# Batch 1's x on SyncE's queue, 1 KB pieces of x for every batch, and three more staging buffers in the first layer

## The chip, the cores and the metric

The kernel runs on one core of a Trainium2 chip. The metric is the device time of one execution in microseconds. Engines by their names in the profile: PE is TensorE, DVE is VectorE, ACT is ScalarE, POOL is GpSimd, SP is SyncE (which here only issues DMAs).

## What is computed

Four batches of attention between 512 tokens and 32 state rows (8 heads of 64), read in both directions, then two feed-forward layers over all 2304 rows:

```python
a  = softmax(scale * x @ state.T);  xread = a  @ state      # per batch and head
a2 = softmax(scale * state @ x.T);  sread = a2 @ x
x1 = concat(xread, sread)                                   # 4 batches x (512 + 32) rows, 512 wide
h  = x1 @ w_in;  x2 = (h - tanh(h)) @ w_out                 # 512 -> 2048 -> 512
h  = x2 @ w2_in; out = (h * tanh(softplus(h))) @ w2_out
```

The four weight matrices come as 64-bit floats, 8 MB each, so every tile of 128x512 weights is a load of 512 KB that has to be converted on the chip.

## The kernel before, in words

**Weights.** `load_next` (lines 161 to 170) issues one load of 512 KB on SyncE's queue into a staging buffer; there are three (pool `stage`). `conv_steps` (line 172) converts a loaded tile in three steps: ScalarE reads the high words (tile `w`), ScalarE reads the low words (tile `r`) and then the next load is issued, and VectorE joins the two. Where a weight is used in three matmuls of the fp32r type (all but the first `PLAIN` = 3 tiles of w_out), `split` makes a high part on ScalarE and a low part on VectorE (`wh`, `wl`; `gh`, `gl` for activations). Loads of the first layer alternate: four tiles of w_in, then w_in and w_out in turn, 32 in all.

**First layer, batch by batch.** The state is multiplied into w_in first (`sw`, `sw_first`; tiles `swh`, `swl`), so that the attention weights a (transposed and split: `ath`, `atl`, by `at_a_hi` and `at_a_lo`) meet it directly. For each batch, step t of 16 does `up_x` (6 matmuls into `h`, then tanh into `t` on ScalarE, a subtraction on VectorE, a split) and, three steps later (`LA`), `down_x` (12 matmuls into the four `acc` banks; 4 plain ones for the first three tiles). In batch 0's 16 steps the weights are converted too, two tiles a step; after every fourth step `sw` needs four new tiles of w_in. After batch 0 all weights stay in place. The second layer follows, block by block.

**Start.** `FIRST_LOADS` is the order of the first loads on SyncE's queue: `s` and `t` are the two states, a digit is one quarter of a batch's x (0 to 3 batch 0), `w` a weight tile. `FIRST_STEPS` is an order written out by hand: while `Pinned.on` is set, TensorE, ScalarE and VectorE each execute their instructions strictly in the order of this list, up to the bar; behind it the scheduler orders them by priority and readiness. The letters stand for the functions in `steps` (line 892): `x`/`X` transpose and copy a quarter of batch 0's x, `p`/`P` of batch 1's; `c`/`C` and `q`/`Q` are the scores and their copies for batches 0 and 1; `t m b e u v y` the softmax of batch 0; `h`/`l` the attention weights transposed and split; `f` the product of state and w_in; `w` one step of a weight's conversion; `k` matmuls on zeros; `L` issues batch 1's x on GpSimd's queue behind VectorE's last instruction.

**Layout of x.** A quarter of a batch's x holds two heads. Batch 0's comes in 1 KB pieces (four tokens of a head), so that one transposed 128x128 block holds two tokens of one head, on partitions 0 to 63 and 64 to 127. `sc_first` therefore needs each head's state on both halves of the partitions, in `SB` and, swapped, in `SX`. Batches 1 to 3 come in pieces of 256 bytes on GpSimd's queue, with the two heads side by side, and `sc_m` takes matmuls of 512 columns.

**Slots.** 97 slots of 128x512 are handed out by `get` and taken back by `put`, oldest first.

## Time and profile before

| | us |
|---|---|
| median of 3 runs | 756.31 (755.75 to 756.71) |
| the profiled execution, its own time | 755.38 |
| its span, first to last instruction | 753.6 |
| TensorE busy in the span | 732.3 |
| VectorE / ScalarE / GpSimd busy | 537.0 / 417.6 / 16.2 |

The profile is one execution on the core. A row of a timeline has its start and duration in us; behind a row, in brackets, stands how long the engine had been idle and what released it. `L56` is the line of the helper that records every operation, so the tiles' names tell which operation it is: `out<-in`. In groups, `busy, mean ns | idle before <-releaser` follow the count.

### The profile page before, as it was taken

Reading aid. Unit: us, or ns where it says so; the run is one execution under the profiler, and the core shown is the slowest. Engines: PE = TensorE matmul, PEld = TensorE weight load, DVE = VectorE, ACT = ScalarE, POOL = GpSimd, SP = SyncE. Lnnn points to the kernel's source line nnn. Section 1 sums busy time; section 2 is a strip of 40 time slices with the busy share of each in tenths; the row PEclk is TensorE's granted clock in tenths of the full one; section 3 lists DMA queues with packets and bytes.
Section 4 is the critical chain, followed back from the end, with each engine's and each line's share of the span. In section 5 each row is a group of like instructions: output and inputs, shape, how many; then the busy total and the mean of one; then the engine's idle time right before and its main releaser. Section 6 shows DMA issues by size and latency. Waiting matters only on the chain.

```text
span 753.6 us, 10473 instructions
## 1 busy us (share of the span) xinstructions
PE 732.3 (97%) x4108; PEld 593.1 (79%) x4108; DVE 537.0 (71%) x989; ACT 417.6 (55%) x779; POOL 16.2 (2%) x18
## 2 busy tenths in 40 slices
PE   7889899999999999999999999999999999999997
PEld 5546687678777788777888888888888888899996
DVE  3657865664447444677698987878887888788896
ACT  4789844544545543688774644445444454545563
POOL 3000020000200000000000000000000000000000
PEclk9899999999999999999999999999999999999999
DMA  8477720000200200253410000100010000100100
GB/s 246 146 239 242 230 56 1 2 1 30 84 29 29 85 29 29 78 159 128 140 57 1 0 1 2 56 1 0 1 57 0 1 1 0 57 1 1 43 1 28
DMA packets 16400, 43.13 MB, mean 57 GB/s; under 512 B 2656, under 2 KB 5728, under 8 KB 16352
## 3 DMA queue, kind: packets, MB, share of 16 engines
q1 hardware_dynamic: 15392, 39.33, 16.2%
q0 software_dynamic: 960, 3.15, 1.7%
q8 instruction: 32, 0.52, 0.3%
q14 instruction: 16, 0.13, 0.1%
HBM read 38.01 MB, written 4.46 MB: 56 GB/s over the span
## 4 chain that ended last, share of the span: by engine, by line
PE 87%; DMA 5%; ACT 4%; DVE 3%; issue 0%; POOL 0%; SPq 0%; ACTq 0%
PE acc L56 45%; PE h L56 36%; DMA st<-in_moe_w_in_dram 3%; DMA x<-in_x_dram 2%; PE swp L56 2%; ACT w L56 1%; ACT r L56 1%; DMA st<-in_moe_w_out_dram 1%; PE srd L56 1%; PE xtp L56 1%; DVE swl L56 1%; PE atp L56 1%; PE e2p L56 1%; ACT gh L56 0%; PE sct L56 0%; ACT t L56 0%
## 5 line engine op out<-in xcount | busy, mean ns | idle before, releaser
L56 PE MATMUL h<-yl,wh 128*128 128x512 f32 (+2 forms) x320 | 114.4, 358 | 0.0
L56 PE MATMUL h<-yh,wl 128*128 128x512 f32 (+2 forms) x320 | 114.4, 358 | 0.0
L56 PE MATMUL h<-yh,wh 128*128 128x512 f32 (+2 forms) x320 | 114.3, 357 | 0.0
L56 PE MATMUL acc<-wl,gh 128*128 128x512 f32 x288 | 112.5, 391 | 0.0
L56 PE MATMUL acc<-wh,gh 128*128 128x512 f32 x288 | 112.5, 390 | 0.0
L56 PE MATMUL acc<-wh,gl 128*128 128x512 f32 x288 | 112.4, 390 | 0.0
L56 ACT ACTIVATE er<-er 128x512 f32<-128x512 f32 (+2 forms) x136 | 75.8, 557 | 42.7 <-DVE er L56 40.6
L56 PE MATMUL acc<-gh,wh 128*128 128x512 f32 x244 | 99.0, 406 | 0.0
L56 ACT ACTIVATE er<-h 128x512 f32<-128x512 f32 (+2 forms) x68 | 35.5, 522 | 109.5 <-PE h L56 108.4
L56 PE MATMUL acc<-gh,wl 128*128 128x512 f32 x244 | 95.5, 391 | 0.0
L56 PE MATMUL acc<-gl,wh 128*128 128x512 f32 x244 | 95.1, 390 | 0.0
L56 DVE TENSOR_TENSOR t<-h,t 128x512 f32<-128x512 f32 x68 | 46.8, 688 | 65.5 <-ACT t L56 65.3
L56 DVE SCALAR_TENSOR_TENSOR er<-er 128x512 f32<-128x512 f32 (+2 forms) x136 | 81.3, 598 | 4.7
L56 ACT ACTIVATE t<-h 128x512 f32<-128x512 f32 x68 | 40.6, 597 | 70.8 <-PE h L56 70.5
L56 PEld LDWEIGHTS h<-yh,wh 128*128 128x128 f32 x320 | 60.3, 188 | 8.9
L56 PEld LDWEIGHTS h<-yl,wh 128*128 128x128 f32 x320 | 60.3, 188 | 8.9 <-DVE yl L56 0.4
L56 PEld LDWEIGHTS h<-yh,wl 128*128 128x128 f32 x320 | 60.3, 188 | 7.5
L56 PEld LDWEIGHTS acc<-wh,gl 128*128 128x128 f32 x288 | 54.0, 188 | 11.5
L56 PEld LDWEIGHTS acc<-wh,gh 128*128 128x128 f32 x288 | 54.1, 188 | 11.4 <-ACT t L56 0.8
L56 PEld LDWEIGHTS acc<-wl,gh 128*128 128x128 f32 x288 | 54.1, 188 | 10.2
L56 PEld LDWEIGHTS acc<-gh,wh 128*128 128x128 f32 x244 | 45.8, 188 | 18.9 <-issue 6.5
L56 DVE SCALAR_TENSOR_TENSOR w<-w,r 128x512 uint32<-128x512 uint32 x64 | 44.0, 689 | 21.6 <-ACT r L56 17.1
(100 smaller groups left out, 1204.3 us busy)
## 6 DMA issues: line engine op xcount, KB each, us to landing
st<-in_moe_w_in_dram SPq DMA_DIRECT2D x32, 512.0 KB, 4.4
st<-in_moe_w_out_dram SPq DMA_DIRECT2D x32, 512.0 KB, 4.1
out_dram<-o SPq DMA_DIRECT2D x16, 256.0 KB, 2.2
x<-in_x_dram POOLq DMA_DIRECT2D x12, 256.0 KB, 4.3
x<-in_x_dram SPq DMA_DIRECT2D x4, 256.0 KB, 4.0
stt<-in_state_dram SPq DMA_DIRECT2D x2, 128.0 KB, 5.1
out_dram<-o SPq DMA_DIRECT2D x4, 64.0 KB, 1.7
```

The costliest lines, as they stand in the source:

```text
L56: i = fn(*args, **kw)
```

## The change

Batch 1's x is loaded on SyncE's queue behind the first two weights and the second state, and the x of all batches comes in 1 KB pieces; batches 2 and 3 stay on GpSimd's queue. All scores are computed as batch 0's were, with the swapped state `SX` now for both states in a slot, copied by VectorE. The hand-written start is reordered: weight 0 and 1 are converted earlier, and `f` is divided into `f` (matmul and high part) and `g` (low part). The slots fall to 91; the memory of six of them makes three staging buffers `wide`, which take loads 3, 4, 5, then 9, 10, 11 and so on of the first layer's weights, so that six loads go out at the start instead of three. When batch 1's layer starts, `widen` hands their six halves out as slots; `get` takes a half first for 32-bit float tiles.

```diff
--- before.py
+++ after.py
@@ -15,6 +15,7 @@
 AX = mybir.AxisListType
 LA = 3
+WIDE = 3
 RESERVE = 10
 E20 = 485165195.40979
 REBIAS = 2.0 ** -112
@@ -28,10 +29,12 @@
-FIRST_LOADS = "s0123wwwt"
+FIRST_LOADS = "s0123wwt4567wwww"
 FIRST_STEPS = """
-    k4 s0 x0 X0 x1 X1 x2 X2 x3 X3 L c0 C0 C1 k2 t0 m0 t1 b0 w0 w0 m1 e0 w1 b1 w0 k8 e1 w1 u0 p0
-    P0 p1 P1 f0 v0 y0 p2 P2 u1 v1 h0 p3 P3 y1 k4 h1 l0 w1 l1 w2 q1 Q0 Q1 | f1 w2 w2 f2 w3 w3 w3 f3
+    k4 s0 x0 X0 x1 X1 x2 X2 x3 X3 w0 w0 c0 C0 C1 k2 w0 t0 m0 t1 w1 w1 f0 b0 p0 P0 m1 e0 p1 P1 b1
+    p2 e1 P2 u0 p3 P3 v0 y0 k6 w2 u1 v1 w2 h0 q1 y1 k2 h1 g0 l0 w1 l1 Q0 Q1 | f1 g1 w2 f2 g2
+    w3 w3 w3 f3 g3
 """
 BLOCKS = [4, 4, 4, 3, 2]
@@ -101,16 +104,24 @@
     slots = ctx.enter_context(tc.tile_pool(name="slots", bufs=1))
     psum = ctx.enter_context(tc.tile_pool(name="psum", bufs=1, space=bass.MemoryType.PSUM))
-    NSLOT = 97
-    free = deque(range(NSLOT))
+    NSLOT = 97 - 2 * WIDE
+    free, halves = deque(range(NSLOT)), deque()
+    wide = [slots.tile([128, 1024], F32, tag=f"v{i}", name="wide") for i in range(WIDE)]
     def get(name, dtype=F32, newest=False):
+        if halves and dtype == F32:
+            return halves.popleft()
         i = free.pop() if newest else free.popleft()
         return Unit(slots.tile([128, 512], dtype, tag=f"k{i}", name=name), i)
     def put(*units):
         for u in units:
-            free.append(u.slot)
+            if u.slot is None:
+                halves.append(u)
+            else:
+                free.append(u.slot)
     ps_n = [0]
     banks = ["s0", "s1", "a0", "a1", "a2", "a3", "h0", "h1"]
@@ -124,11 +135,12 @@
     XS = get("xst")
     xst = XS.t.rearrange("p (k n) -> p k n", k=KD)
-    SX = misc.tile([128, KD * NS], F32, name="sx")
-    def head(b, k, i):
+    SX = get("sx")
+    def head(b, k, i, half=None):
         c = (b * KD + k) * NS
-        return SB.t[i * 64:(i + 1) * 64, c:c + NS]
+        p = i if half is None else half
+        return (SB if p == i else SX).t[p * 64:(p + 1) * 64, c:c + NS]
     def by_head(name, b, rhs):
@@ -155,6 +167,7 @@
     last = [None]
+    loads = [-1]
     pending = deque()
     raws = {}
@@ -162,7 +175,11 @@
         if not pending:
             return
         key, src = pending.popleft()
-        t = stage.tile([128, 1024], U32, tag="st", name="st")
+        loads[0] += 1
+        if key[0] in ("w1i", "w1o") and loads[0] % (3 + WIDE) >= 3:
+            t = wide[loads[0] % (3 + WIDE) - 3].bitcast(U32)
+        else:
+            t = stage.tile([128, 1024], U32, tag="st", name="st")
         if key[:2] == ("w1i", 0):
             nc.sync.dma_start(out=t.rearrange("p (k c) -> p k c", k=KD), in_=src)
         else:
@@ -240,25 +257,17 @@
     X, A, AT = {}, {}, {}
     XT, SC, ET = {}, {}, {}
-    def load_x(b, ks=range(KD), after=None):
+    def load_x(b, ks=range(KD)):
         for k in ks:
             u = get("x", newest=b > 1)
-            if b:
-                dma = nc.gpsimd.dma_start(
-                    out=u.t.rearrange("p (r h d) -> p r h d", r=4, h=2),
-                    in_=x[b, 2 * k:2 * k + 2].rearrange("h (p r) d -> p r h d", r=4),
-                )
-                if after is not None:
-                    order(dma.ins, after, mybir.DependencyClass.Sync)
-            else:
-                nc.sync.dma_start(
-                    out=u.t.rearrange("p (h c) -> p h c", h=2),
-                    in_=x[b, 2 * k:2 * k + 2].rearrange("h (p r) d -> p h (r d)", r=4),
-                )
+            (nc.gpsimd if b > 1 else nc.sync).dma_start(
+                out=u.t.rearrange("p (h c) -> p h c", h=2),
+                in_=x[b, 2 * k:2 * k + 2].rearrange("h (p r) d -> p h (r d)", r=4),
+            )
             X[b, k] = u
     def x_tile(b, k, i, r):
-        c = r * 128 + i * 64 if b else i * 256 + r * 64
+        c = i * 256 + r * 64
         return X[b, k].t[:, c:c + 64]
     P = {}
@@ -283,44 +292,35 @@
         xt_t(b, k)
         xt_c(b, k)
-    def sc_first():
-        P["c"] = [side_bank("sct") for _ in range(2)]
+    def sc_m(b):
+        P["c", b] = [side_bank("sct") for _ in range(2)]
         before = None
         for i in range(2):
             for k in range(KD):
                 for e in range(2):
                     with tc.high_priority() if before else nullcontext():
                         mm = TE.matmul(
-                            out=P["c"][e][k * NS:(k + 1) * NS, i * 256:(i + 1) * 256],
-                            lhsT=head(0, k, i) if e == i
-                            else SX[e * 64:(e + 1) * 64, k * NS:(k + 1) * NS],
-                            rhs=XT[0, k].t[e * 64:(e + 1) * 64, i * 256:(i + 1) * 256],
+                            out=P["c", b][e][k * NS:(k + 1) * NS, i * 256:(i + 1) * 256],
+                            lhsT=head(b, k, i, e),
+                            rhs=XT[b, k].t[e * 64:(e + 1) * 64, i * 256:(i + 1) * 256],
                             start=True,
                             stop=True,
                         ).ins
                     if before:
                         order(mm, before)
                     before = mm
-        put(*(XT.pop((0, k)) for k in range(KD)))
-    def sc_first_c(i):
-        SC[0, i] = get("scs")
+        put(*(XT.pop((b, k)) for k in range(KD)))
+    def sc_c(b, i):
+        SC[b, i] = get("scs")
         for e in range(2):
             evac(
-                SC[0, i].t.rearrange("p (q e n) -> p q e n", q=2, e=2)[:, :, e, :],
-                P["c"][e][:, i * 256:(i + 1) * 256].rearrange("p (q n) -> p q n", q=2),
+                SC[b, i].t.rearrange("p (q e n) -> p q e n", q=2, e=2)[:, :, e, :],
+                P["c", b][e][:, i * 256:(i + 1) * 256].rearrange("p (q n) -> p q n", q=2),
                 e,
             )
-    def sc_m(b):
-        P["c", b, 0], P["c", b, 1] = by_head("sct", b, [[XT[b, k].t for k in range(KD)]])
-        put(*(XT.pop((b, k)) for k in range(KD)))
-    def sc_c(b, j):
-        SC[b, j] = get("scs")
-        AC.activation(out=SC[b, j].t, in_=P.pop(("c", b, j)), func=ACTF.Copy)
     def at_scores(b):
         sc_m(b)
@@ -487,13 +487,17 @@
                 put(SB)
     def sw_first(f):
-        ps = by_head("swp", 0, [[w1i_tile(0, k, f) for k in range(KD)]])
+        P["f", f] = ps = by_head("swp", 0, [[w1i_tile(0, k, f) for k in range(KD)]])
         for j in range(2):
             if f == 0:
                 SW[0, 0, j] = (get("swh", F32R), get("swl", F32R))
+            h = SW[0, 0, j][0].t[:, f * 128:(f + 1) * 128]
+            AC.activation(out=h, in_=ps[j], func=ACTF.Copy)
+    def sw_first_lo(f):
+        for j, ps in enumerate(P.pop(("f", f))):
             h, l = (u.t[:, f * 128:(f + 1) * 128] for u in SW[0, 0, j])
-            AC.activation(out=h, in_=ps[j], func=ACTF.Copy)
-            V.tensor_tensor(out=l, in0=ps[j], in1=h.bitcast(F32), op=ALU.subtract)
+            V.tensor_tensor(out=l, in0=ps, in1=h.bitcast(F32), op=ALU.subtract)
     def mm3p(o, lh, ll, rh, rl, start, stop):
@@ -853,12 +857,10 @@
                 in_=ps[p].rearrange("p (e i n) -> p e i n", i=2, n=NS)[:, :, i, :],
                 func=ACTF.Copy,
             )
-            if g == 0:
-                AC.activation(
-                    out=SX[p].rearrange("p (k n) -> p k n", n=NS),
-                    in_=ps[p].rearrange("p (e i n) -> p e i n", i=2, n=NS)[:, :KD, 1 - i, :],
-                    func=ACTF.Copy,
-                )
+            V.tensor_copy(
+                out=SX.t[p, g * 256:(g + 1) * 256].rearrange("p (e n) -> p e n", n=NS),
+                in_=ps[p].rearrange("p (e i n) -> p e i n", i=2, n=NS)[:, :, 1 - i, :],
+            )
         put(u)
     nc.scalar.preload_act_table_set("exp_and_others")
@@ -891,10 +893,11 @@
     steps = {
         "x": lambda k: xt_t(0, k), "X": lambda k: xt_c(0, k), "s": lambda j: state_t(j, st[j]),
-        "c": lambda j: sc_first(), "C": sc_first_c, "t": lambda j: sc_t(0, j),
+        "c": lambda j: sc_m(0), "C": lambda j: sc_c(0, j), "t": lambda j: sc_t(0, j),
         "m": lambda j: sc_max(0, j), "b": lambda j: sc_sub(0, j), "e": lambda j: sc_exp(0, j),
         "u": lambda j: nm_sum(0, j), "v": lambda j: nm_rec(0, j), "y": lambda j: nm_mul(0, j),
         "h": lambda j: at_a_hi(0, j), "l": lambda j: at_a_lo(0, j), "f": sw_first,
+        "g": sw_first_lo,
         "w": conv_first, "k": keep_warm, "p": lambda k: xt_t(1, k), "P": lambda k: xt_c(1, k),
         "q": sc_m, "Q": lambda j: sc_c(1, j),
     }
@@ -904,13 +907,17 @@
         if key == "|":
             for e in (TE, AC, V):
                 e.floor, e.on = e.last, False
-        elif key == "L":
-            load_x(1, after=V.recent)
         else:
             steps[key[0]](int(key[1:]))
     put(warm)
     at(4, lambda: state_t(1, st[1]))
     banks[2:] = []
+    def widen():
+        for t in wide:
+            put(*(Unit(t[:, h * 512:(h + 1) * 512], None) for h in range(2)))
+    at(start[1], widen)
     def up(q):
         if q[0] == "x":
```

## Rows read from the trace of the kernel before

**Rows 1.** The page: totals of the engines, and the span in 40 equal slices.

```profile
PE 732.3 (97%) x4108; PEld 593.1 (79%) x4108; DVE 537.0 (71%) x989; ACT 417.6 (55%) x779; POOL 16.2 (2%) x18
...
PE   7889899999999999999999999999999999999997
...
DMA  8477720000200200253410000100010000100100
```

**Rows 2.** Busy time by window: engine busy us (instructions), PEclk, DMA share, GB/s.

```profile
0.00:10.00 10.00, 7.92 (x72) 5.84 (x72) 1.87 (x3) 3.56 (x7) 1.42 (x7) 1.00 0.79 243
...
7.50:10.00 2.50, 2.22 (x36) 1.00 (x36) 0.69 (x1) 0.30 (x1) 0.73 (x1) 1.00 1.04 347
...
10.00:25.00 15.00, 11.52 (x110) 9.20 (x108) 9.53 (x20) 8.48 (x17) 4.55 (x4) 0.77 0.66 171
...
12.50:15.00 2.50, 1.55 (x13) 1.15 (x11) 2.47 (x5) 2.17 (x4) 2.05 (x2) 1.00 0.91 178
...
20.00:25.00 5.00, 4.88 (x53) 3.92 (x52) 3.56 (x8) 2.80 (x5) 0.00 (x0) 0.71 0.02 8
...
25.00:86.10 61.10, 51.55 (x283) 32.69 (x268) 42.38 (x71) 53.87 (x104) 0.00 (x0) 1.00 0.72 232
...
86.10:753.60 667.50, 661.28 (x3664) 545.39 (x3662) 483.25 (x897) 351.69 (x654) 10.22 (x8) 1.00 0.11 36
```

**Rows 3.** The chain of waits, 0 to 100 us: its shares, then pieces (start us, us, what).

```profile
by line: DMA st<-in_moe_w_in_dram 20.6%; DMA x<-in_x_dram 12.6%; ACT w L56 8.8%; ACT r L56 8.5%; DMA st<-in_moe_w_out_dram 8.2%; PE acc L56 8.0%; PE h L56 4.1%; ACT gh L56 3.2%; PE xtp L56 2.6%; ACT t L56 2.1%; POOL x L247 1.9%; issue 1.7%;
...
11.16 7.82 DMA x<-in_x_dram
...
88.29 2.76 PE acc L56 x12
...
91.05 1.36 PE h L56 x6
```

**Rows 4.** Timeline of TensorE: start us, us, operation [idle before <-releaser].

```profile
7.58 0.66 PE L56 MATMUL xtp<-ident,x 128*128 128x128 f32 x4 [0.41 <-DMA x<-in_x_dram]
...
13.88 0.63 PE L56 MATMUL xtp<-ident,x 128*128 128x128 f32 x4 [0.46 <-DMA x<-in_x_dram]
...
19.11 1.09 PE L56 MATMUL xtp<-ident,x 128*128 128x128 f32 x4 [0.94 <-DMA x<-in_x_dram]
...
25.12 0.50 PE L56 MATMUL h<-ath,swh 128*128 128x512 f32 x1
...
80.08 1.09 PE L56 MATMUL swp<-w,sbt 64*32 64x512 f32 x16 [1.32 <-DVE w L56]
...
85.81 0.66 PE L56 MATMUL sc<-ident,scs 128*128 128x128 f32 x4 [1.69 <-DVE swl L56]
...
86.22 0.48 PE L56 MATMUL h<-ath,swh 128*128 128x512 f32 x1
```

**Rows 5.** Timelines of GpSimd, VectorE and SyncE, 9 to 28 us.

```profile
9.27 5.28 POOL L247 DMA_DIRECT2D x<-in_x_dram  x4 [7.97 <-DVE xt L56]
...
10.15 0.76 DVE L56 COPY scs<-sct 128x256 f32<-128x256 f32 x2 [1.18 <-PE sct L56]
...
27.08 0.34 SPq L169 DMA_DIRECT2D st<-in_moe_w_out_dram  x1
```

**Rows 6.** Groups of ScalarE's instructions, 10 to 25 us and 25 to 86.1 us.

```profile
L56 ACT ACTIVATE xt<-xtp 128x512 f32<-128x512 f32 x4 | 2.4, 592 | 3.7 <-PE xtp L56 3.7
...
L56 ACT ACTIVATE w<-st 128x512 f32<-128x512 f32 x29 | 19.8, 682 | 7.0 <-DMA st<-in_moe_w_in_dram 6.4 <-DMA st<-in_moe_w_out_dram 0.4
```

**Rows 7.** Waits of SyncE's queue, 0 to 95 us: us in total, times, longest.

```profile
SPq L169 <- ACT r L56: 57.4, 30, 11.4
```

**Rows 8.** Timelines of ScalarE and VectorE about 120 us.

```profile
120.42 0.60 ACT L56 ACTIVATE t<-h 128x512 f32<-128x512 f32 x1 [1.45 <-PE h L56]
...
122.44 0.69 DVE L56 TENSOR_TENSOR gl<-t,gh 128x512 fp32r<-128x512 f32 x1 [0.70 <-ACT gh L56]
```

## The prediction, made before the changed kernel ran

> **What bounds the kernel now.** I read the page's totals and slices first [rows 1]. TensorE is busy for 732.3 of 753.6 us, and its line of tenths is at 9 nearly everywhere except in the first five slices, some 90 us. In those same slices the DMA line stands at 7 and 8. So what can be gained cheaply lies ahead of 90 us. The windows confirm it [rows 2]: from 86.1 us to the end TensorE is busy for 661.28 of 667.50 us, 6.2 us idle in all, while from 25 to 86.1 us it is busy for 51.55 of 61.10 us, 9.55 us idle. The chain of waits over the first 100 us [rows 3] then says which resource it is: the loads of the first layer's weights hold 20.6% and 8.2% of it, x another 12.6%, and TensorE's matmuls for acc and h only 8.0% and 4.1%. This stretch is led by transfers, in two parts.
>
> *Part one, up to 25 us.* The first up-projection matmul starts at 25.12 us [rows 4]. What it waits for is a line of small steps written out by hand, and batch 1's four transposes stand in the middle of that line. They are held by batch 1's x: the piece of the chain that begins at 11.16 us is one x transfer of 7.82 us [rows 3], and the transposes start at 13.88 and 19.11 us, each released by a landing [rows 4]. GpSimd issues these four loads only at 9.27 us [rows 5]. ScalarE meanwhile sits idle for 3.7 us ahead of the copies of those transposes [rows 6]. While the 256-byte pieces move, the DMA engines are nearly full (0.91) yet carry 178 GB/s, against 347 GB/s in the window before them [rows 2]. Then, from 20 to 25 us, the engines carry 8 GB/s at a share of 0.02 [rows 2]: all three staging buffers are full, and SyncE's next load goes out at 27.08 us [rows 5], since ScalarE reaches weights 2 and 3 late.
>
> *Part two, 25 to 86.1 us.* The DMA share is 0.72 [rows 2]. SyncE waits 30 times, 57.4 us together, for ScalarE's second read of a staging buffer (r) [rows 7], then the load needs time to land, and ScalarE in turn idles 7.0 us ahead of its first read (w), 6.8 us of it named as those loads [rows 6]. That is a ring of three buffers in which each side waits for the other.
>
> **The change, part by part.**
>
> *Front.* Batch 1's x moves from GpSimd's queue, with a wait on VectorE, to SyncE's, ahead of weights 2 and 3. Ahead of it go state 0 and 1 (128 KB each), batch 0's x (1 MB) and two weights (512 KB each), 2.36 MB; the trace moved 243 GB/s times 10 us, 2.43 MB, by 10.0 us [rows 2]. The 1.05 MB of x then takes 3.0 us at 347 GB/s, so 13.0 us. Completion comes about 1.1 us behind the bytes: by 7.5 us 1.56 MB had moved [rows 2], 0.38 MB more than batch 0's x needs with its state, and its last tile released TensorE only at 7.58 us [rows 4]. So x is in by about 14 us instead of some 20. Weights 2 and 3 and the next two follow in the queue at 1.5 us each, so weight 2 lands at about 16 us, where ScalarE wants it by the same reckoning. The x transfer so leaves the chain, and the next limit is VectorE: from 10 to 25 us it executes 20 instructions, 9.53 us [rows 2], and the new order holds the same 20 before the first up-projection. From the scores' copies at 10.15 us [rows 5] that is 19.7 us at the earliest, a gain of 5.4 us. I don't expect all of it, because TensorE's granted clock is at its lower level for a part of this stretch (mean 0.77 from 10 to 25 us [rows 2]), after transposes with waits between them, and the new stretch is as sparse, with fewer warming matmuls (14 instead of 18). At the lower level four transposes take 1.09 us instead of 0.63 [rows 4], 0.46 us each time, and about three such groups (the last x tile and the two of the weights a) lie on the path: 1.4 us. **Term one: 4.0 us**, with bounds of 0 (weight 2 stands ahead of the copies of a on ScalarE, so a late landing there would give it all back) and 5.4.
>
> *Six staging buffers.* Load n+6 may go when weight n is read, instead of n+3. The first six are issued at once, which fills the empty window at 20 to 25 us. Are the transfers fast enough? The stretch moves 232 GB/s times 61.1 us, 14.2 MB; at 347 GB/s that is 41 us [rows 2], less than ScalarE's 53.87 us of work in the same stretch. So ScalarE is late next, not the DMA: its idle time there is 61.10 less 53.87, 7.2 us, of which 7.0 stand ahead of w [rows 6]. It can't all go: three times in this stretch TensorE needs a projection of the state by the next four weight tiles, and waits for VectorE to form the weight (1.32 us at 80.08) or for its split (1.69 us at 85.81) [rows 4]; these are latencies through three engines. I take 6.0 of the 7.0 us. **Term two: 6.0 us**, with bounds of 0 and 9.55, all of TensorE's idle time (ScalarE could give more than 7.2 only by doing fewer conversions ahead of need).
>
> Here a rule speaks against the buffers. The trace's row is the DMA share of 0.72 and the 57.4 us of SyncE's waits [rows 2, 7]. The Trainium skill, page "DMA: Bandwidth & Descriptors", section "Anatomy of one DMA — SWDGE (gpsimd) path", puts a transfer at about 2.0 us plus its bytes over 436 GB/s. An estimate from that page: 3.2 us for 512 KB, so three in flight would already ask for some 490 GB/s, more than the fabric has, and the three new buffers would bring nothing. The rows disagree: the buffer is held not by its transfer but by the conversion queued on ScalarE. The sum goes by the rows; the rule's outcome is the second rival.
>
> *Scores in halves.* For batches 1 to 3 the 16 score matmul instructions of 512 columns become 32 of 256. The columns for each tile of the array are the same, so I count nothing, though it is TensorE's own time; batch 0 has this form already, and the bounds are a gain or a loss of half a microsecond, about one more set of four transposes in all [rows 4]. ScalarE gives half of the copies to VectorE, whose busy share after 86.1 us is 483 of 667 us [rows 2]: covered. So are the swapped state copies, which go from ScalarE to VectorE; without that cover they would cost VectorE under a microsecond.
>
> *Slots.* 97 slots become 91, one of them taken by the swapped state; six return as halves when batch 1's layer starts. Batches 2 and 3's x are loaded three steps before use: nothing, and their GpSimd issue gets shorter. The six halves are taken first and again as soon as they are free: cost 0 taken, see the third rival.
>
> *Sum.* 4.0 + 6.0 = 10.0 us. The profiled execution took 755.38 us (span 753.6), so 745.4; the median of the three runs, 756.31, is 0.93 above it, so **746.3 us**.
>
> **The rivals.**
>
> 1. *All idle time goes.* Term one at 5.4 and term two at 9.55: 756.31 - 14.95 = 741.4 us. For it: TensorE's work and ScalarE's fit side by side. Against: ScalarE is busy for 53.87 of 61.10 us, and its order would have to be perfect.
> 2. *The buffers bring nothing.* Deeper loads let conversions crowd ahead of the tanh of the same step on ScalarE, which runs strictly in order; TensorE's 9.55 us stay under another name. Only term one is left: 752.3 us. For it: ScalarE at 88%. Against: its idle is nearly all put to DMA. By the page's rule above the time is the same.
> 3. *Slower: the halves bind.* From batch 1's layer on, a step's t may sit in the half that the step before has just freed, so its tanh waits for the last read of the older t. That runs from 120.42 to 122.44 + 0.69 = 123.13 us, 2.7 us [rows 8], while a step of TensorE is 2.76 + 1.36 = 4.1 us [rows 3]. It decides when that chain exceeds 4.1 us, as when conversions queue between; if each of 51 steps (17 to 67) then lost 0.3 us it would be 15 us: 761.6 us.
> 4. *It doesn't do what it says:* a weight in front of the scores' copies on ScalarE comes late and takes back term one, and rival 2 holds as well: 756.3 us.
>
> **How the numbers follow.** The forecast has 0.72, the rivals 0.08, 0.12, 0.06 and 0.02. The range is 741.4 to 751.6: it reaches from both terms' upper bounds to a gain of 4.7 us, which is one term lost and the other kept in part, and leaves out rivals 2, 3 and 4 (0.20). A measurement here can tell about 0.2% (1.5 us) from no change. Faster: 0.72 + 0.08 + 0.12 = 0.92; same 0.02; slower 0.06.
>
> **What would show it.** Right: batch 1's x lands by about 14 us; no empty DMA window before all first-layer weights are in; the first up-projection near 21 us; the one that stands at 86.22 [rows 4] near 76; ScalarE almost never idle ahead of w; the rest of the span shifted whole. Wrong: the first h after 24 us, or TensorE's idle time between it and the point of 86.22 still near 9 us (rival 2), or more than the present 6.2 us idle behind that point, ahead of tanh (rival 3).

## The result, and the profile after

| | before | after |
|---|---|---|
| median of 4 runs, us | 756.51 (755.75 to 757.41) | 746.01 (745.84 to 746.06) |
| ratio, 95% interval | | 0.986 (0.9843 to 0.9877) |
| the profiled execution, us | 755.38 | 746.04 |
| its span, us | 753.6 | 744.3 |

The forecast was 746.3 us, in a range of 741.4 to 751.6. The medians further down leave out one execution of E10 (909.92 us), one of E11 (2578.03) and one of the kernel before on the chip of E5 to E8 (1879.08), which lie far off the others of the same kernel. The page of the changed kernel, totals of the engines and slices, beside [rows 1]:

```profile
PE 729.4 (98%) x4148; PEld 591.0 (79%) x4148; DVE 541.4 (73%) x999; ACT 416.2 (56%) x777; POOL 6.6 (1%) x14
...
PE   7999999999999999999999999999999999999997
...
PEclk9999999999999999999999999999999999999999
DMA  9885110002100110453310000100010000100100
```

TensorE's line is at 9 from the second slice to the last but one, where it had 8 in three of the next four. The DMA line is fuller in the first slices and falls to 5 and 1 in slices 4 and 5, where it stood at 7: the first layer's weights are in earlier. GpSimd's busy time falls from 16.2 to 6.6 us with the shorter and fewer issues of x.

Busy time of each engine by window (columns as in [rows 2]); the second and third window are cut at the first and at the thirteenth up-projection; an up-projection is six matmuls into `h`, and the first of them is the row that marks it:

```profile
10.00:25.00 15.00, 12.66 (x159) 8.63 (x159) 12.58 (x27) 11.77 (x28) 0.00 (x0) 1.00 0.92 320
...
20.00:25.00 5.00, 4.87 (x67) 2.90 (x66) 3.52 (x8) 4.15 (x11) 0.00 (x0) 1.00 0.60 214
...
21.12:76.32 55.20, 51.22 (x277) 32.82 (x269) 46.35 (x79) 54.27 (x107) 0.00 (x0) 1.00 0.69 238
...
76.32:744.30 667.98, 661.04 (x3693) 545.80 (x3691) 483.24 (x897) 350.38 (x649) 5.90 (x8) 1.00 0.11 35
```

TensorE's timeline, the rows that answer to [rows 4]:

```profile
12.58 2.88 PE L59 MATMUL xtp<-ident,x 128*128 128x128 f32 x16
...
18.44 0.40 PE L59 MATMUL sct<-xt,sbt 64*32 64x256 f32 x1 [1.20 <-DVE swl L59]
...
19.66 0.71 PE L59 MATMUL warm<-warm 128*128 128x128 f32 x4
20.21 0.60 PE L59 MATMUL atp<-ident,a 128*128 128x128 f32 x4
...
21.12 0.50 PE L59 MATMUL h<-ath,swh 128*128 128x512 f32 x1
...
75.36 0.66 PE L59 MATMUL sc<-ident,scs 128*128 128x128 f32 x4 [1.68 <-DVE swl L59]
...
76.32 0.39 PE L59 MATMUL h<-ath,swh 128*128 128x512 f32 x1
...
302.81 0.66 PE L59 MATMUL ysp<-ident,ys 128*128 128x128 f32 x4 [0.88 <-ACT ys L59]
```

The three points that cut the span read so:

| | before | after | difference |
|---|---|---|---|
| first up-projection | 25.12 | 21.12 | -4.00 |
| from it to the thirteenth | 61.10 | 55.20 | -5.90 |
| from there to the end | 667.38 | 667.98 | +0.60 |
| span | 753.6 | 744.3 | -9.30 |

From 20 to 25 us, where the DMA engines carried 8 GB/s [rows 2], they carry 214, and TensorE's granted clock is 1.00 from 10 to 25 us, where its mean was 0.77. Batch 1's sixteen transposes are now one row without a wait, from 12.58 us; SyncE issues their x from 5.12 us on, and each load lands 7.0 to 7.3 us later, the last at about 14.6 us, where the forecast had 14. The chain of waits over the first 100 us names no transfer of x any more and puts ScalarE's two reads at its head, where [rows 3] had the loads. Its two pieces at 18.44 us are what stands ahead of the first up-projection:

```profile
by line: ACT r L59 15.9%; ACT w L59 15.8%; PE acc L59 14.4%; PE h L59 7.3%; DMA st<-in_moe_w_in_dram 6.2%; ACT t L59 5.5%; ACT wh L59 5.1%; ACT gh L59 3.7%; ACT swh L59 2.9%; DVE a L59 2.8%; issue 2.5%; DVE sm L59 2.1%; SPq L263 1.9%; PE sc
...
18.44 1.29 PE sct L59 x29
19.73 0.64 PE warm L59 x4
```

Groups of ScalarE's instructions from 25 to 86.1 us, beside [rows 6]: ahead of its first reads (`w`) it idled 7.0 us, 6.8 of it for loads, and now 0.9 us, none of it for a load.

```profile
L59 ACT ACTIVATE w<-st 128x512 f32<-128x512 f32 x14 | 9.8, 702 | 0.9 <-DVE gl L59 0.9
...
L59 ACT ACTIVATE w<-wide 128x512 f32<-128x512 f32 x13 | 9.0, 689 | 0.0
L59 ACT ACTIVATE t<-h 128x512 f32<-128x512 f32 x13 | 8.0, 612 | 2.2 <-PE h L59 2.1
```

### The profile page after: what moved, and what is told of

The parts are those of the page before. It is cut to its first block, busy times and chain, and to the rows that moved or that the text cites. A ratio compares the mean times of both kernels' runs of the same rounds, so it can differ in the third digit from the quotient of the medians.

```text
span 744.3 us, 10607 instructions
## 1 busy us (share of the span) xinstructions
PE 729.4 (98%) x4148; PEld 591.0 (79%) x4148; DVE 541.4 (73%) x999; ACT 416.2 (56%) x777; POOL 6.6 (1%) x14
## 3 DMA queue, kind: packets, MB, share of 16 engines
q1 hardware_dynamic: 16480, 40.38, 16.2%
## 4 chain that ended last, share of the span: by engine, by line
PE 87%; ACT 7%; DVE 3%; DMA 1%; issue 1%; SPq 0%; ACTq 0%
PE acc L59 46%; PE h L59 36%; ACT w L59 2%; ACT r L59 2%; PE swp L59 2%; PE srd L59 1%; DMA st<-in_moe_w_in_dram 1%; DVE swl L59 1%; ACT t L59 1%; ACT swh L59 1%; ACT wh L59 1%; PE e2p L59 1%; PE sct L59 1%; ACT gh L59 1%; PE xtp L59 0%
## 5 line engine op out<-in xcount | busy, mean ns | idle before, releaser
L59 DVE TENSOR_SCALAR er<-er 128x512 f32<-128x512 f32 (+2 forms) x68 | 25.8, 379 | 44.2 <-ACT er L59 44.1
L59 DVE TENSOR_TENSOR t<-h,t 128x512 f32<-128x512 f32 x48 | 33.0, 688 | 34.0 <-ACT t L59 34.0
L59 PEld LDWEIGHTS acc<-gh,wl 128*128 128x128 f32 x244 | 45.8, 188 | 10.2 <-issue 0.4
```

The lines of the kernel that those rows point to most:

```text
L59: i = fn(*args, **kw)
```

## The experiments

The theory: the front gained because batch 1's x left the chain, the stretch behind it because six buffers keep ScalarE supplied. The first rival: the buffers bring nothing. E1 to E4, E5 to E8 and E9 to E12 ran on one chip each, on which the kernel before took 756.33, 755.0 and 755.2 us (medians); each ratio is to these executions. So medians from two of these chips can differ by a microsecond without any edit, and what is smaller is read from the traces. The four marks below come from one profiled execution each: VectorE's start on the scores' copies of batch 0, the first up-projection, the thirteenth, and the stretch between the last two, in us.

| kernel | median | ratio to before (95%) | copies | first up | 13th up | stretch |
|---|---|---|---|---|---|---|
| before | 756.51 | | 10.15 | 25.12 | 86.22 | 61.10 |
| after | 746.01 | 0.986 (0.9843 to 0.9877) | 9.91 | 21.12 | 76.32 | 55.20 |
| E1 three buffers | 752.83 | 0.9964 (0.9944 to 0.9984) | 13.05 | 23.61 | 86.05 | 62.44 |
| E2 buffers alone | 754.09 | 0.9978 (0.9965 to 0.9992) | 10.42 | 29.73 | 84.85 | 55.12 |
| E3 256-byte pieces | 747.99 | 0.9898 (0.9873 to 0.9923) | 12.56 | 23.37 | 78.45 | 55.08 |
| E4 low part early, no warming | 744.72 | 0.9854 (0.9834 to 0.9875) | 10.30 | 18.98 | 74.72 | 55.74 |
| E5 four buffers | 751.24 | 0.9951 (0.9935 to 0.9967) | 10.42 | 20.99 | 78.20 | 57.21 |
| E6 eight buffers | 746.92 | 0.9889 (0.9875 to 0.9903) | 10.90 | 21.46 | 76.43 | 54.97 |
| E7 split on GpSimd | 745.55 | 0.9872 (0.9856 to 0.9888) | 10.21 | 21.09 | 75.49 | 54.40 |
| E8 x on GpSimd's queue | 753.14 | 0.9973 (0.9962 to 0.9983) | 10.44 | 27.14 | 82.26 | 55.12 |
| E9 three edits | 743.02 | 0.9837 (0.9825 to 0.985) | 11.36 | 19.92 | 73.58 | 53.66 |
| E10 three buffers again | 752.45 | 0.9962 (0.9948 to 0.9976) | 11.71 | 22.27 | 82.87 | 60.60 |
| E11 low part alone | 744.27 | 0.9852 (0.9835 to 0.9869) | 11.17 | 19.74 | 75.56 | 55.82 |
| E12 softmax later | 745.16 | 0.9865 (0.9852 to 0.9877) | 11.07 | 21.64 | 74.78 | 53.14 |

The copies start between 9.9 and 13.1 us at the same order of loads, since batch 0's x lands at different moments (last section). So fronts are compared from the copies on: 14.97 us before, 11.21 after.

### The buffers: E1, E10, E5, E6

E1 and its repeat E10 take the three buffers away, so that the six slots come back, and keep all else of the change:

```diff
-WIDE = 3
-FIRST_LOADS = "s0123wwt4567wwww"
+WIDE = 0
+FIRST_LOADS = "s0123wwt4567w"
```

> The changed kernel with three staging buffers (none that turn into slots, 97 slots, three first loads), its new start and x as changed. Theory (two terms that add: the start 4.0 us, the buffers 5.9 us): the first up-projection matmul stays at 21.1 us, the stretch from it to the thirteenth up-projection is 61.1 us again instead of 55.2, and the time is about 752.0 us. Rival (the buffers bring nothing; weights that come early because the start is shorter do it all): the stretch stays at 55.2 us and the time at 746.0 us.

> The run with three staging buffers once more, since its profiled execution had batch 0's x late. Theory: first up-projection at 21.1 us, stretch 61 us, thirteenth at 82 us, time 751 to 753 us. Rival: the new start does not hold with three buffers and the first up-projection is at 23.5 us again.

Measured: 752.83 and 752.45 us. In E1's profiled execution batch 0's last x tile was late (TensorE waited 2.27 us for it), and this execution took 757.62 us, so E10 is the one to read. From the copies to the first up-projection it takes 22.27 - 11.71 = 10.56 us: the front's gain of 4 us is there without the buffers. The stretch is back at 60.60 us, and ScalarE's idle time ahead of `w` with it, as the group of E10 from 20 to 88 us shows:

```profile
L59 ACT ACTIVATE w<-st 128x512 f32<-128x512 f32 x29 | 19.6, 675 | 6.0 <-DMA st<-in_moe_w_in_dram 3.6 <-DMA st<-in_moe_w_out_dram 2.1
```

Six buffers are thus worth 60.60 - 55.20 = 5.4 us in the trace, and 6.4 us by the medians (752.45 against 746.01; the intervals of the ratios lie apart). Not all of it is waiting, as the window of E10's stretch shows:

```profile
22.27:82.87 60.60, 52.49 (x277) 34.10 (x269) 44.85 (x76) 54.33 (x105) 0.00 (x0) 0.97 0.70 226
```

TensorE is busy for 52.49 us of it at a mean granted clock of 0.97, against 51.22 us at 1.00 in the changed kernel. So 4.1 of the 5.4 us are waits (8.11 us of idle time against 3.98), and 1.3 us go with the clock. The medians hold the clock too: the six executions of E1 and E10 with a mean of 0.998 took 750.39 to 751.87 us, still 4.3 us or more above those of the changed kernel at 0.999 and 1.00 (745.84 to 746.06). E2 below adds the buffers to the kernel before with the clock at 1.00 in both stretches, and there the stretch falls by 6.0 us.

The Trainium skill's page "DMA: Bandwidth & Descriptors", section "Anatomy of one DMA — SWDGE (gpsimd) path", has a transfer that GpSimd issues take a fixed time and its bytes over a rate; an estimate from it said that three buffers already keep the fabric full. The runs disagree. These loads are SyncE's and land 4.1 and 4.4 us after issue (w_out and w_in, medians of the kernel before) where the estimate had 3.2, and a buffer is held on while its conversion queues on ScalarE, which is time in no transfer.

E5 and E6 change the number:

```diff
-WIDE = 3
-FIRST_LOADS = "s0123wwt4567wwww"
+WIDE = 1
+FIRST_LOADS = "s0123wwt4567ww"
```

```diff
-WIDE = 3
-FIRST_LOADS = "s0123wwt4567wwww"
+WIDE = 5
+FIRST_LOADS = "s0123wwt4567wwwwww"
```

> The changed kernel with one buffer that turns into slots instead of three (four staging buffers, four first loads). Theory: most of the buffers' gain is in the loads of the start, so one buffer more gives a part of it only: first up-projection at 21.1 us, the stretch to the thirteenth 57 to 59 us, 748 to 750 us. Rival (the fourth buffer is enough, since ScalarE is the bound as soon as it does not wait): 746 us.

> The changed kernel with five such buffers (eight staging buffers, eight first loads). Theory (ScalarE is the bound of the stretch now: it is busy for nearly all of it and no longer idle ahead of w): the stretch stays at 55.2 us, the time at 745.5 to 746.5 us. Rival (the loads are still late): 1 to 3 us faster, 743 to 745 us.

The stretch over three, four, six and eight buffers is 60.60, 57.21, 55.20 and 54.97 us, and TensorE's idle time in it, which leaves E10's lower clock out, 8.11, 6.05, 3.98 and 3.83 us. The fourth buffer brings half of what six bring, the seventh and eighth nothing that the time shows; E6's 746.92 us is even a little over what was expected. E5's time of 751.24 us is over what was expected too, although its stretch is where it was expected: behind the thirteenth up-projection it took 670.50 us against 667.98, the window below. Two waits of the `acc` matmuls, 0.9 us for ScalarE's `gh` and 0.6 us for VectorE, stand there that the changed kernel does not have; the rest of the 2.5 us, and why four buffers bring it, stays open.

```profile
78.20:748.70 670.50, 661.71 (x3693) 545.68 (x3691) 482.39 (x897) 348.81 (x648) 5.89 (x8) 1.00 0.10 34
```

### The place in the queue and the pieces: E2, E8, E3

E2 is the kernel before with the buffers alone (`wide`, `halves`, `widen`); x keeps GpSimd's queue, its pieces and the old order.

```diff
+WIDE = 3
-FIRST_LOADS = "s0123wwwt"
+FIRST_LOADS = "s0123wwwtwww"
```

> The kernel before, its start and its x in 256-byte pieces on GpSimd's queue, with the six staging buffers alone and six first loads. Theory: the first up-projection stays at 25.1 us or comes up to 1 us later (three more weights share the DMA engines with batch 1's x), the stretch to the thirteenth is 55.2 us, the time 750.5 to 751.5 us. Rival (the buffers bring nothing by themselves): 756.3 us, or more by the later x.

Measured: 754.09 us. The stretch, 55.12 us, is that of six buffers. But the first up-projection came at 29.73 us, 4.6 us later than before, where a microsecond at most was expected. TensorE's timeline of E2:

```profile
18.82 1.09 PE L57 MATMUL xtp<-ident,x 128*128 128x128 f32 x4 [5.13 <-DMA x<-in_x_dram]
...
22.67 1.09 PE L57 MATMUL xtp<-ident,x 128*128 128x128 f32 x4 [0.30 <-DMA x<-in_x_dram]
...
29.73 0.50 PE L57 MATMUL h<-ath,swh 128*128 128x512 f32 x1
```

Three more weights, 1.57 MB, are in the queue when GpSimd issues x; at the 347 GB/s of [rows 2] they are 4.5 us of transfers. The third tile of x released TensorE 3.6 us later than before (22.67 against 19.11); another 1.0 us is lost behind it, where, after TensorE's wait of 5.13 us, the granted clock was 0.50 from 20 to 25 us, which is the lower of its two levels (1.2 GHz), and 0.70 on average from 25 to 30 us (before: 0.71 and 1.00). The buffers alone so bring 2.2 us (756.33 - 754.09), and the two parts of the change aren't independent: the buffers pay in full only if x doesn't have to wait behind their loads.

E8 is the changed kernel with batch 1's x back on GpSimd's queue, in 1 KB pieces, released as before:

```diff
-FIRST_LOADS = "s0123wwt4567wwww"
+FIRST_LOADS = "s0123wwtwwww"
...
-    k4 s0 x0 X0 x1 X1 x2 X2 x3 X3 w0 w0 c0 C0 C1
+    k4 s0 x0 X0 x1 X1 x2 X2 x3 X3 L w0 w0 c0 C0 C1
...
-            (nc.gpsimd if b > 1 else nc.sync).dma_start(
+            dma = (nc.gpsimd if b else nc.sync).dma_start(
...
+            if after is not None:
+                order(dma.ins, after, mybir.DependencyClass.Sync)
...
+        elif key == "L":
+            load_x(1, after=V.recent)
```

> The changed kernel with batch 1's x on GpSimd's queue again, released as before behind the last copy of batch 0's x, but in 1 KB pieces. Theory (its place ahead of the weights counts, apart from the size of the pieces): it starts at 11 us with some 1.6 MB of weights still queued on the other queue and shares the engines with them, lands at 17 to 18.5 us instead of 14.5, the first up-projection is at 24 to 25 us and the time 749 to 750 us. Rival (1 KB pieces alone give the gain): 746 to 747 us.

Measured: 753.14 us, first up-projection at 27.14, 16.70 us behind the copies against 11.21. TensorE's and GpSimd's timelines of E8:

```profile
16.57 0.82 PE L59 MATMUL xtp<-ident,x 128*128 128x128 f32 x4 [3.89 <-DMA x<-in_x_dram]
...
20.93 1.09 PE L59 MATMUL xtp<-ident,x 128*128 128x128 f32 x4 [0.32 <-DMA x<-in_x_dram]
```

```profile
9.56 3.00 POOL L263 DMA_DIRECT2D x<-in_x_dram  x4 [8.26 <-DVE xt L59]
```

So where x is issued decides the front, and with six buffers it is worth more than was expected: 5.5 us here (16.70 - 11.21). Issued from 9.56 us on, x holds TensorE until 20.93 us, while the weights of SyncE's queue move on the same DMA engines: from 12 to 20 us GpSimd's queue takes a share of 0.37 of them and SyncE's 0.68. The Trainium skill says so on the page "DMA: Bandwidth & Descriptors", section "Issuing engines are not separate DMA queues": transfers of different issuers run on the same engines and interleave. The trace agrees. E8 undoes the queue and the moment of issue (9.56 us against 5.12) together, and a part of the 5.5 us is the granted clock, 0.69 and 0.63 in the two windows from 15 to 25 us where the changed kernel had 1.00. What the new order of the steps brings by itself, with x where it was and three buffers, was not tried.

E3 keeps the order and queue of the change and brings back the 256-byte pieces (with `x_tile`, `sc_first`, `sc_m` and `SX` as before):

```diff
-            (nc.gpsimd if b > 1 else nc.sync).dma_start(
-                out=u.t.rearrange("p (h c) -> p h c", h=2),
-                in_=x[b, 2 * k:2 * k + 2].rearrange("h (p r) d -> p h (r d)", r=4),
+                (nc.gpsimd if b > 1 else nc.sync).dma_start(
+                    out=u.t.rearrange("p (r h d) -> p r h d", r=4, h=2),
+                    in_=x[b, 2 * k:2 * k + 2].rearrange("h (p r) d -> p r h d", r=4),
```

> The changed kernel, start, queue and buffers as changed, but x of batches 1 to 3 in 256-byte pieces as before, with the scores in matmuls of 512 columns. Theory that the size of the pieces counts: batch 1's 1.05 MB take 5.9 us at 178 GB/s instead of 3.0, its last tile and weight 2 land 2 to 3 us later, the first up-projection is at 23 to 24 us, the time 748 to 749 us. Rival (only the place in the queue counts; the low rate came from two queues sharing the engines): 21.1 us and 746.0 us.

Measured: 747.99 us, from 745.79 to 751.06 in six executions. The profiled one, 750.91 us, began late (copies at 12.56 us), and its front lost next to nothing: 10.81 us from the copies to the first up-projection. SyncE took 8.11 us to issue the four loads, against 4.06 in the changed kernel, and TensorE waited 0.58 us for a tile of batch 1's x, at 16.94 us, while the engines carried 190 GB/s at a share of 0.86 in the small pieces:

```profile
12.50:15.00 2.50, 2.50 (x31) 2.14 (x32) 2.35 (x5) 1.95 (x5) 0.00 (x0) 0.86 0.86 190
```

The late start hid what the slower landing would have cost. Another 2.7 us of this execution lie behind the thirteenth up-projection (670.65 against 667.98 us), a wait of 1.57 us for VectorE among them; their cause stays open. On GpSimd's queue the size does count: E2 and E8 issue x there at the same moment (9.54 and 9.56 us) behind as many weights, and its third tile released TensorE at 22.67 us in E2, with 256-byte pieces, and at 19.53 in E8, with 1 KB. What the larger pieces bring on SyncE's queue, 0 to 3 us by times and ratios, stays open.

### What is late next: E7, E12

The prediction said that ScalarE would be late next, and the stretch seems to bear that out: it is busy for 54.27 of 55.20 us. E7 takes the high part of w_out's split off it:

```diff
-        dst[key[1:]] = split(w.t, name="w")
+        if key[0] == "w1o":
+            h, l = get("wh", F32R), get("wl", F32R)
+            nc.gpsimd.tensor_copy(out=h.t, in_=w.t)
+            V.tensor_tensor(out=l.t, in0=w.t, in1=h.t.bitcast(F32), op=ALU.subtract)
+            dst[key[1:]] = (h, l)
+        else:
+            dst[key[1:]] = split(w.t, name="w")
```

> The changed kernel with the high part of the split of the first layer's second weights (wh) copied by GpSimd instead of ScalarE. Theory (ScalarE is the bound of the stretch): it is freed of 10 to 12 copies at 0.52 us each, and the thirteenth up-projection comes 2 to 4 us earlier: 742 to 744 us. Rival (the bound is the chain through the engines for the state's products, or GpSimd's copies are late or slow VectorE down): 746 us or slower.

Measured: 745.55 us. The window of E7 between its first and its thirteenth up-projection:

```profile
21.09:75.49 54.40, 51.42 (x277) 32.81 (x270) 46.25 (x79) 49.17 (x95) 9.27 (x12) 1.00 0.70 245
```

ScalarE has 5.1 us less to do, and the stretch is 0.8 us shorter. So ScalarE's work as a whole is not what bounds it; the expectation missed. GpSimd's copies took 0.61 to 1.17 us each, ScalarE's 0.63 (median), so they may have given something back; that was not separated. TensorE's 4.0 us of idle time in the stretch (55.20 - 51.22) are single waits, the largest the 1.68 us at 75.36 us above, where the scores' transposes of batch 1 (`sc`) stand behind VectorE's `swl`. E12 leaves all the work where it is and moves batch 1's softmax by one step, so that these transposes come behind the thirteenth up-projection:

```diff
-        at(11 + j, lambda j=j: at_exp(1, j))
-        at(12 + j, lambda j=j: at_norm(1, j))
+        at(12 + j, lambda j=j: at_exp(1, j))
+        at(13 + j, lambda j=j: at_norm(1, j))
```

> The changed kernel with batch 1's softmax one step later (steps 12 and 13 instead of 11 and 12). Theory (what is left of TensorE's idle time is not ScalarE's load but single waits in TensorE's strict order, here the transposes of batch 1's scores that wait 1.7 us for the PSUM bank of the state's product while two matmuls and the thirteenth up-projection stand behind them): the up-projection comes 1.0 to 1.6 us earlier, 744.4 to 745.0 us. Rival (the up-projection waits for the same split anyway): 746.0 us.

TensorE's timeline and the window of the stretch in E12:

```profile
74.78 0.50 PE L59 MATMUL h<-ath,swh 128*128 128x512 f32 x1
...
75.89 0.50 PE L59 MATMUL h<-ath,swl 128*128 128x512 f32 x1 [0.39 <-DVE swl L59]
...
76.92 0.60 PE L59 MATMUL sc<-ident,scs 128*128 128x128 f32 x4
```

```profile
21.64:74.78 53.14, 50.74 (x273) 32.33 (x265) 44.41 (x76) 52.94 (x105) 0.00 (x0) 1.00 0.72 245
```

What is left of the wait is 0.39 us, and the thirteenth up-projection is 1.5 us earlier, with ScalarE busy for 52.94 of 53.14 us. But the transposes and that wait now lie behind the mark, and there E12 takes 1.2 us more than the changed kernel's 667.98:

```profile
74.78:744.00 669.22, 661.90 (x3696) 546.21 (x3696) 485.33 (x900) 351.58 (x651) 5.90 (x8) 1.00 0.11 35
```

From the first up-projection to the end E12 takes 722.36 us, the changed kernel 723.18 and E7 722.41. Measured: 745.16 us, just above the range that was expected; the ratios of E7 and E12, 0.9872 and 0.9865, don't lie below the changed kernel's 0.986, so these gains rest on the traces. Another place in TensorE's order for one group of transposes is worth as much, 0.8 us, as 5.1 us of ScalarE's work, and E7 gains on the same wait: it is 0.65 us there.

### Where the rest of the front is: E4, E11

After's rows show TensorE waiting 1.20 us at 18.44 us for VectorE's `swl` before it may start batch 1's scores (`sct`), which stand ahead of the transposes of a. `side_bank` hands out seven banks of PSUM in turn; f takes two, batch 1's transposes four, those of a one, and so the scores get f's two again, whose low part (`swl`) has to be read out first. E11 moves this low part (`g0`) ahead; E4 does that and drops the last warming matmuls (`k2`), which E11 keeps.

```diff
-    p2 e1 P2 u0 p3 P3 v0 y0 k6 w2 u1 v1 w2 h0 q1 y1 k2 h1 g0 l0 w1 l1 Q0 Q1 | f1 g1 w2 f2 g2
+    p2 e1 P2 u0 p3 P3 v0 y0 g0 k6 w2 u1 v1 w2 h0 q1 y1 h1 l0 w1 l1 Q0 Q1 | f1 g1 w2 f2 g2
```

> The changed kernel with two steps of the start moved: the low part of the first product of state and weights (g0) right behind y0, and without the two warming matmuls ahead of the second transposition of a (k2). Theory: in the changed kernel batch 1's scores wait 1.2 us for g0, since both use the same PSUM banks, and the warming matmuls hold 0.6 us more; the first up-projection comes at 20.1 to 20.4 us instead of 21.1 and the time is 745.0 to 745.3 us. Rival (the later y1 on VectorE takes it back, or TensorE's clock falls without the two): 746.0 us or more.

> The changed kernel with g0 behind y0 alone, the two warming matmuls k2 kept. Theory (the wait of batch 1's scores for the PSUM banks of the first product): the scores' 1.2 us wait for the low part is gone, and 0.5 to 1.0 us of the 1.3 us that the two edits gained together remain: 745.0 to 745.5 us. Rival (the warming matmuls were the cost): 746.0 us.

Measured: 744.72 and 744.27 us. TensorE's timelines, E4 first, then E11:

```profile
16.99 0.40 PE L59 MATMUL sct<-xt,sbt 64*32 64x256 f32 x1
...
18.60 0.63 PE L59 MATMUL atp<-ident,a 128*128 128x128 f32 x4 [0.52 <-DVE a L59]
18.98 0.48 PE L59 MATMUL h<-ath,swh 128*128 128x512 f32 x1
...
21.50 0.50 PE L59 MATMUL h<-ath,swh 128*128 128x512 f32 x1
```

```profile
17.70 0.40 PE L59 MATMUL sct<-xt,sbt 64*32 64x256 f32 x1
...
18.72 0.71 PE L59 MATMUL warm<-warm 128*128 128x128 f32 x4
19.35 0.63 PE L59 MATMUL atp<-ident,a 128*128 128x128 f32 x4
19.74 0.48 PE L59 MATMUL h<-ath,swh 128*128 128x512 f32 x1
```

The wait ahead of `sct` is gone in both, and from the copies to the first up-projection they take 8.68 and 8.57 us against 11.21. Not all of these 2.6 us are the bank: the changed kernel's execution also waited 0.64 us for ScalarE's copies of the scores (last part), and with the same start and no such wait E5, E6, E10 and E12 take 10.56 to 10.57 us. So the bank is worth 2.0 us, and the warming matmuls cost nothing: without them, E4's transposes wait 0.52 us for VectorE. Some of it is lost again right behind: in E4 the second up-projection starts 2.52 us behind the first (21.50 us), in the changed kernel 1.97 (23.09), and the thirteenth comes 64.42 us behind the copies against 66.41. Without the 0.64 us of the other wait some 1.3 us are kept, which is also what the medians differ by (746.01 - 744.72).

### All three: E9

E9 joins the edits of E4, E7 and E12.

> The changed kernel with the three edits together: g0 early and no second warming matmuls, wh on GpSimd, batch 1's softmax one step later. If they act on different waits, their gains add: 1.3 + 0.5 + 1.3 us, 742.4 to 743.5 us. If the later ones remove the same idle time of TensorE, 744 us or more.

Measured: 743.02 us, ratio 0.9837 (0.9825 to 0.985), the shortest time of this study. Its stretch, and the thirteenth up-projection at 73.58 us although its copies began 1.45 us later than after's:

```profile
19.92:73.58 53.66, 51.30 (x283) 32.70 (x282) 46.32 (x80) 49.30 (x95) 9.33 (x11) 1.00 0.73 259
```

From the copies to the thirteenth up-projection it is 62.22 us against 66.41. It did not run on the same chip as the changed kernel, and the intervals of the two ratios overlap (0.9843 to 0.985); that it is shorter rests on the trace as much as on the times. The single edits, about 1.3 us for the low part and 0.8 us each for the other two, add up to about the 3.0 us of the medians, as was expected; each by itself is read from the traces.

## Why the prediction was right

**Which resource binds.** Right. x left the chain, ScalarE's idle time for loads went from 6.8 us to nothing, and where one part was undone, its loss came back: rival 2 put the whole change at 752.3 us, and it is the kernel without the buffers, E10, that takes 752.45. The estimate from the Trainium skill's page "DMA: Bandwidth & Descriptors", section "Anatomy of one DMA — SWDGE (gpsimd) path", gave the same 752.3 us; the runs disagree with it (E10 above). One reading was loose: in the first five slices the DMA line has 8, 4, 7, 7, 7 [rows 1], not 7 and 8 throughout; nothing was worked out from it.

**Term one, 4.0 us.** Measured 4.00, and 3.76 from the copies on, but one of its steps was wrong. The floor of VectorE, 5.4 us, was to be cut by 1.4 us since TensorE would transpose at its lower clock level (0.5, 1.2 GHz). The granted clock was 1.00, the upper level of 2.4 GHz, in the whole of 10 to 25 us, so nothing was lost that way. What took its place are two waits of TensorE: 0.64 us for ScalarE's copies of the scores, and 1.20 us of `sct` for VectorE's `swl`, with the scores' own 1.2 us (18.44 to 19.66) behind it, in front of the transposes of a. In E11 neither stands, and its front is 2.6 us shorter. So the size of the term came out by luck, for another reason than the one given; and a part of what it measures is the clock, up from 0.77 to 1.00, which no run separates. Nor was 5.4 us the upper bound that the text called it: all 20 instructions of VectorE were counted ahead of the first up-projection, and with another order E4 gets there 8.68 us behind the copies, less than the 9.53 us of that count. The first of the two waits is rival 4's mechanism, small: weight 0 came late on ScalarE, whose copies of the scores began 0.8 us behind VectorE's.

```profile
9.58 0.66 ACT L59 ACTIVATE w<-st 128x512 f32<-128x512 f32 x1 [1.65 <-DMA st<-in_moe_w_in_dram]
...
10.70 0.64 ACT L59 ACTIVATE scs<-sct 128x256 f32<-128x256 f32 x2
```

```profile
9.91 0.76 DVE L59 COPY scs<-sct 128x256 f32<-128x256 f32 x2 [1.18 <-PE sct L59]
```

```profile
11.12 1.09 PE L59 MATMUL sc<-ident,scs 128*128 128x128 f32 x8 [0.64 <-ACT scs L59]
```

These are ScalarE's, VectorE's and TensorE's timelines of the changed kernel.

**Term two, 6.0 us.** Measured 5.90, by the mechanism that was named; "the buffer is held not by its transfer but by the conversion queued on ScalarE" is what E2, E10, E5 and E6 show. The step "ScalarE is late next" was half right. ScalarE is nearly always busy, but E7 shows that its work as a whole is not what sets the stretch's end. The 4 us that stay are waits in TensorE's order, of the two kinds that the prediction named (1.32 and 1.69 us of [rows 4]); E12 shortens one. SyncE's waits for ScalarE's second read fell from 57.4 us [rows 7] to 37.9 (waits of SyncE's queue, 0 to 95 us): the issuer still waits for buffers, but now with more loads ahead of their reader.

```profile
SPq L186 <- ACT r L59: 37.9, 24, 5.5
```

**The parts costed at nothing.** From the thirteenth up-projection to the end the span is 0.60 us longer. TensorE's idle time behind that point is 6.94 us (667.98 - 661.04), and was 6.2, and one new wait, 0.88 us at 302.81 us for ScalarE's `ys`, is more than the difference. The runs say where it comes from. E10 has it too, with no buffer that turns into slots; E2, with the buffers and the 91 slots alone, and E3, with x and the scores of batches 1 to 3 as before, have not. So it goes with the new form of x and the scores, which was costed at nothing, and not with the slots: E2 takes 667.55 us behind its thirteenth up-projection, against 667.38 before. Rival 3 would have shown there as 15 us; the halves do not bind. These are the row of E10 and the window of E2:

```profile
310.98 0.66 PE L59 MATMUL ysp<-ident,ys 128*128 128x128 f32 x4 [0.88 <-ACT ys L59]
```

```profile
84.85:752.40 667.55, 661.30 (x3661) 545.28 (x3659) 482.47 (x893) 352.24 (x650) 10.25 (x8) 1.00 0.11 35
```

**The sum.** Against the profiled execution's own time, 755.38 us, a gain of 10.0 was predicted and 9.34 came (746.04). The median was then set 0.93 us above the profiled execution, as it stood before; after the change the two agree within 0.03 us. The two errors are of opposite sign, and that 746.3 fell as close to 746.01 as it did is luck.

## What to carry to other kernels

A ring of buffers is sized by how long each buffer is held, the wait for its reader included, and not by the time of its transfer: count the idle time of the reader that is put down to loads, and add buffers until it is gone (here 6.0 us with three buffers, 1.6 with four, none with six). Deeper loads are new traffic ahead of whatever is issued later, so put the transfer that the first steps need in front of them in the same queue; done alone, the buffers gave most of their gain back here (4.6 of 6.0 us). And an engine that is busy for 98% of a stretch need not bound it with all of its work: before moving its work, look at the single waits of the engine that sets the end, and try another place in the order first.

## What the runs showed of the hardware that was not expected

**Landing of the first loads.** Batch 0's x, issued alike, let VectorE begin the scores' copies at 9.91 us in one kernel and at 13.05 in another. In E1 TensorE waited 2.27 us for its last tile; the clock granted in the 5 us behind that has a mean of 0.74, between the two levels of 1.2 and 2.4 GHz (0.5 and 1.00), though TensorE was busy for 4.99 of them:

```profile
10.00:15.00 5.00, 4.99 (x64) 2.54 (x63) 2.64 (x5) 3.04 (x6) 0.00 (x0) 0.74 1.08 339
```

**Scatter.** E1's twelve executions lie between 750.39 and 757.62 us, those of the changed kernel between 745.84 and 746.06, of E4 between 744.46 and 745.08. The time goes with the mean granted clock: E1's three executions at 0.998 took 750.39 to 750.87 us, its one at 0.989 757.62, and the kernel before on the same chip took 753.04 us at 0.999 and 757.34 and 758.32 at 0.991. All four of the changed kernel were at 0.999 or 1.00. So a part of what the change gains in the median, beside executions of the kernel before of which most were at 0.993 to 0.995, goes with the clock; no run separates the clock from the waits ahead of which or behind which it fell.

**Rate by the size of the pieces.** At much the same share of the DMA engines, packets of 256 bytes moved 190 GB/s (share 0.86, the window of E3 above), packets of 1 KB, x and the first weights, 347 GB/s (1.04, the window from 7.5 us of [rows 2]), and the 4 KB packets of later weights 410 GB/s, in this window of the changed kernel. The 178 GB/s of [rows 2] is a mix: x in 256-byte pieces held 0.70 of the engines' time there, weights 0.21.

```profile
17.50:20.00 2.50, 1.56 (x35) 0.95 (x36) 2.28 (x5) 0.46 (x1) 0.00 (x0) 1.00 1.03 410
```
